# Head sums in one part, the mask on VectorE and an earlier bias transpose in a two-layer transformer kernel

## The chip, the cores and the metric

The kernel runs on one core of a Trainium2 chip. The metric is device time in microseconds (us), the median of several runs. PE is TensorE, DVE is VectorE, ACT is ScalarE, POOL is GpSimd and SP issues most transfers.

## The reference, cut to what matters

Two layers; each is an attention block and a feed-forward block with a residual. 2048 positions, width 1024, 32 heads of 32. The attention is local and dilated: a position looks at 8 keys, 0, 2, ..., 14 positions back.

```python
logits = jnp.einsum("bhsd,bhswd->bhsw", q, kg) * scale      # W = 8 keys per position
logits = jnp.where(mask[None, None, :, :], logits, -1e9)    # keys before the start
attn = _softmax(logits, axis=-1)
o = jnp.einsum("bhsw,bhswd->bhsd", attn, vg)
...
x = x + _A_ref(_layernorm(x), A_wqkv, A_wo)                 # attention
x = x + _B_ref(_layernorm(x), B_w1, B_b1, B_w2, B_b2)       # feed-forward, F = 3584
```

## The kernel before

Positions are handled in 4 groups of 512 per layer. The kernel keeps PE fed: while PE multiplies one group's projections or feed-forward, VectorE prepares another group's attention. For each of 8 chunks `c` VectorE multiplies q with 8 shifted windows of k (`new_prod`, one 128x4096 instruction) and adds the 8 products pairwise. PE then sums over the 4 partitions of each head by a matmul with a 0/1 matrix `smat` (`head_sum`).

```python
def head_sum(n, last=True):
    ...
    first = n % NG == 0
    prod = st[n]["prods"].pop(0)
    for wh in range(2):
        for tb in range(NTT):                       # 4 column groups of PE
            mm(L[tb*H:(tb+1)*H, wh*4:(wh+1)*4, :], lhsT=smat[:], rhs=prod[...],
               start=start, stop=..., tile_position=(0, tb * H))
    if first and last:                              # the mask, as 7 small matmuls
        for w in range(W - 1):
            mm(L[0:H, w, 0:HALO], lhsT=onesrow[:], rhs=maskrow[0:1, w, 0:HALO], ...)

def new_prod(n, c):
    prod = bigp.tile([P, W, T], BF16, name="big")   # 3 buffers
    vec.tensor_tensor(out=prod[:], in0=q chunk c, in1=window of k chunk c, op=ALU.mult)
    ...                                             # add to the others, pairwise
```

With `parts` = 2 (groups 0 and 1 before the change) the products 0 to 3 and 4 to 7 are summed apart, and PE adds the two parts by a second head sum into the same PSUM tile. The order of work is written as stages: a generator issues PE work in units of 8 matmuls, and `sides` hang other work on units. `at(4, f)` issues `f` after unit 4. PE keeps its order; VectorE's order within a stretch is chosen by a scheduler when the program is built, unless `hold()` sets a floor: what is issued later stays behind the last VectorE instruction issued before it.

```python
stage(gen_wo(0, 2))      # output projection of group 0; layernorm tiles 2, 3 are transposed on PE
stage(q2, sides=each(new_prod, 1, 0, 1, 4, 8) + at(3, head_sum, 1, False) + at(4, transpose_late))
...
stage(gen_ffn1(0), sides=at(2, attend, 1) + at(2, spread, 1) + at(2, hold) + ...)

def ln_stats(t, ...):    # VectorE statistics, then two GpSimd instructions
    ...
    vec.bn_aggr(mv[:], stats[:])
    pool.tensor_tensor(out=rstd[:], in0=mv[:, 1:2], in1=eps_t[:], op=ALU.add)
    pool.tensor_tensor(out=rstd[:], in0=rstd[:], in1=mhalf[:], op=ALU.pow)
```

`transpose_late` runs 16 PE transposes: the normalized tiles 2 and 3 of group 0, which the first feed-forward stage needs.

## Time and profile before

| | before |
|---|---|
| time | 1239.82 us (4 runs, 1239.73 to 1239.93) |
| PE busy | 1230.7 us, 99% of the span |
| VectorE busy | 836.5 us, 68% |

The page of the kernel before: the busy row (us, share, instructions), and the chain that ended last, by engine. (In all excerpts from views, lines that do not matter here are left out, also where no dots stand.)

```profile
PE 1230.7 (99%) x5821; PEld 632.5 (51%) x5871; DVE 836.5 (68%) x864; ACT 305.9 (25%) x477; POOL 95.9 (8%) x215
...
PE 99%; issue 0%; ACT 0%; DVE 0%
```

The view of waits, PE alone: who was waited for, us in total, times, longest.

```profile
PE acc L118 <- DVE big L93: 1.1, 1, 1.1
PE acc L118 <- ACT xnT L93: 0.7, 1, 0.7
```

Both waits are in the first 10 us. After that PE hardly stops: the kernel's time is the length of PE's queue.

What the parts of that queue cost is read from start-to-start steps. The timeline of PE (start, length, instruction, operands, count) around group 0's second head sum and mask, the bias transpose, and the stretch at 140 to 151 us:

```profile
36.61 0.18 PE L185 MATMUL acc<-ident,abc 28*128 28x28 bf16 x1
65.20 0.61 PE L118 MATMUL L<-big,smat 128*32 128x512 bf16 x8
65.75 0.33 PE L118 MATMUL L<-maskrow,onesrow 1*32 1x14 bf16 x7
66.01 1.30 PE L118 MATMUL acc<-xnT,wt 128*128 128x512 bf16 x5
147.51 0.61 PE L118 MATMUL L<-big,smat 128*32 128x512 bf16 x8
148.06 1.95 PE L118 MATMUL acc<-xnT,wt 128*128 128x512 bf16 x8
149.84 1.06 PE L215 MATMUL acc<-ident,xn 128*128 128x128 bf16 x16
```

Ordinary 128x512 matmuls start 0.216 us apart. Where a head-sum part stands among them, the stream comes out 0.70 us later, with the mask 0.96 us, around the bias transpose 0.27 us. (Lengths overlap and their ends are modelled, so lengths are not costs.)

The timeline of VectorE and GpSimd before and at the same place. In brackets: idle time before, and what ended it.

```profile
128.62 0.69 DVE L93 TENSOR_TENSOR x<-acc,x 128x512 bf16<-128x512 f32 x1 [2.44 <-PE acc L118]
129.23 2.28 DVE L93 TENSOR_TENSOR big<-qT,kT 128x4096 bf16<-128x4096 bf16 x1
140.70 2.23 DVE L93 TENSOR_TENSOR big<-big 128x4096 bf16<-128x4096 bf16 x1
143.65 0.55 DVE L93 TENSOR_SCALAR xn<-x,mv,rstd 128x1024 bf16<-128x1024 bf16 x1 [0.71 <-POOL rstd L93]
145.90 2.27 DVE L93 TENSOR_TENSOR big<-qT,kT 128x4096 bf16<-128x4096 bf16 x1
149.23 0.55 DVE L93 TENSOR_SCALAR xn<-x,mv,rstd 128x1024 bf16<-128x1024 bf16 x1 [0.93 <-POOL rstd L93]
```

```profile
140.86 2.12 POOL L93 TENSOR_TENSOR rstd<-mv,eps_t 128x1 f32<-128x1 f32 x1 [2.56 <-DVE mv L93]
143.06 0.55 POOL L93 TENSOR_TENSOR rstd<-rstd,mhalf 128x1 f32<-128x1 f32 x1
148.38 0.19 POOL L93 TENSOR_TENSOR rstd<-mv,eps_t 128x1 f32<-128x1 f32 x1 [4.76 <-DVE mv L93]
```

The last normalization (149.23, done at 149.78 us) is ready just before PE's second eight transposes at 149.84 + 0.45 = 150.29 us: half a microsecond of slack. And the same one-column GpSimd addition lasts 2.12 us beside a VectorE addition, 0.19 us without one.

### The profile page before, as it was taken

The page shows a single profiled execution, that of the slowest core. Times are in us where ns is not written, and L with a number is a line of the kernel's source. Part 1 is how long each engine was busy: PE and PEld are TensorE (multiplying, and loading weights), DVE is VectorE, ACT ScalarE, POOL GpSimd, SP SyncE. Part 2 cuts the span into 40 slices and gives each one's busy share as a digit, 9 for nine tenths or more (in the row PEclk, how much of TensorE's full clock was granted, in tenths as well). Part 3 has the DMA queues.
Part 4 walks back from the last instruction along what each step waited for, and adds up shares of the span by engine and source line. Part 5 has one row for each costly group of instructions (what it writes and reads, how often), then busy time and mean ns, then how long its engine had stood idle before and what let it go on. Part 6 is the DMA issues. An engine that isn't in the chain of part 4 may idle for free.

```text
span 1238.2 us, 14051 instructions
## 1 busy us (share of the span) xinstructions
PE 1230.7 (99%) x5821; PEld 632.5 (51%) x5871; DVE 836.5 (68%) x864; ACT 305.9 (25%) x477; POOL 95.9 (8%) x215
## 2 busy tenths in 40 slices
PE   9999999999999999999999999999999999999998
PEld 6666544456444564445644455444654444444444
DVE  7989889996986799337994379843597788012001
ACT  3333252023420144101341023410235001300310
POOL 4010111002000100001000010000001002000000
PEclk9999999999999999999999999999999999999999
DMA  9954564576646556656566565566654568546441
GB/s 300 287 179 139 165 223 134 169 183 211 197 152 205 153 177 169 195 166 178 167 162 196 174 185 157 164 203 198 173 170 134 184 200 205 157 157 195 149 137 54
DMA packets 215328, 219.83 MB, mean 178 GB/s; under 512 B 66066, under 2 KB 184992, under 8 KB 212192
## 3 DMA queue, kind: packets, MB, share of 16 engines
q1 hardware_dynamic: 212592, 208.16, 56.0%
q0 software_dynamic: 2672, 10.76, 2.7%
q8 instruction: 46, 0.75, 0.3%
q14 instruction: 18, 0.15, 0.0%
HBM read 197.40 MB, written 6.29 MB: 165 GB/s over the span
## 4 chain that ended last, share of the span: by engine, by line
PE 99%; issue 0%; ACT 0%; DVE 0%
PE acc L118 99%; PE L L118 0%; PE acc L215 0%; PE L L215 0%; ACT xnT L93 0%; DVE x L93 0%; DVE big L93 0%; PE acc L185 0%
## 5 line engine op out<-in xcount | busy, mean ns | idle before, releaser
L118 PE MATMUL acc<-xnT,wt 128*128 128x512 bf16 (+1 forms) x3376 | 722.4, 376 | 0.7 <-ACT xnT L93 0.7
L118 PEld LDWEIGHTS <-wt 128*128 128x128 bf16 x3376 | 398.0, 119 | 321.2 <-issue 4.3
L118 PE MATMUL acc<-wt,hT 128*128 128x512 bf16 (+1 forms) x1780 | 386.1, 376 | 2.1
L118 PEld LDWEIGHTS <-hT 128*128 128x128 bf16 x1820 | 177.7, 98 | 209.4
L93 DVE TENSOR_TENSOR big<-big 128x2048 bf16<-128x2048 bf16 (+2 forms) x182 | 239.5, 1348 | 1.7
L93 ACT ACTIVATE hT<-acc,b1T 128x512 bf16<-128x512 f32 x224 | 151.6, 687 | 318.5 <-PE acc L118 318.2
L93 DVE TENSOR_TENSOR big<-abc,vT 128x4096 bf16<-128x4096 bf16 x64 | 143.9, 2282 | 48.6 <-DMA abc<-a_d 48.6
L93 DVE TENSOR_TENSOR big<-qT,kT 128x4096 bf16<-128x4096 bf16 x64 | 143.9, 2285 | 24.0 <-ACT kT L93 23.3
L93 DVE TENSOR_TENSOR tmp<-acc,b2bc 128x512 f32<-128x512 f32 x56 | 38.7, 691 | 178.2 <-PE acc L118 174.4
L93 ACT CAST qT<-acc 128x512 bf16<-128x512 f32 x64 | 37.2, 585 | 328.6 <-PE acc L118 328.6
L118 PE MATMUL acc<-wt,oT 128*128 128x512 bf16 x440 | 97.6, 379 | 0.5
L93 DVE BATCH_NORM_STATS2 stats<-x 128x6 f32<-128x512 bf16 x128 | 83.9, 678 | 4.2 <-DMA x<-in_A_x_dram 3.4
L118 PEld LDWEIGHTS <-oT 128*128 128x128 bf16 x448 | 43.8, 98 | 53.1 <-issue 0.3
L93 DVE TENSOR_TENSOR x<-acc,big 128x512 bf16<-128x512 f32 (+1 forms) x9 | 5.7, 632 | 90.0 <-PE acc L118 90.0
L93 ACT CAST vT<-acc 128x512 bf16<-128x512 f32 x64 | 37.5, 586 | 84.9 <-PE acc L118 84.9
L93 ACT CAST kT<-acc 128x512 bf16<-128x512 f32 x64 | 37.5, 585 | 72.1 <-PE acc L118 72.1
L93 POOL TENSOR_TENSOR rstd<-mv,eps_t 128x1 f32<-128x1 f32 x60 | 16.4, 273 | 499.5 <-DVE mv L93 499.4
L93 POOL DMA_DIRECT2D a_d<-a x32 | 18.9, 619 | 406.9 <-DVE a L93 406.9
L93 DVE TENSOR_SCALAR xn<-x,mv,rstd 128x1024 bf16<-128x1024 bf16 x52 | 28.6, 550 | 30.9 <-POOL rstd L93 29.8
L93 DVE TENSOR_TENSOR x<-acc,x 128x512 bf16<-128x512 f32 x64 | 43.0, 671 | 6.3 <-PE acc L118 6.1
L93 DVE TENSOR_TENSOR x<-tmp,x 128x512 bf16<-128x512 f32 x56 | 38.7, 691 | 1.7
L93 POOL TENSOR_TENSOR rstd<-rstd,mhalf 128x1 f32<-128x1 f32 x60 | 33.6, 560 | 4.7
(56 smaller groups left out, 217.3 us busy)
## 6 DMA issues: line engine op xcount, KB each, us to landing
wt<-in_B_w_dram SPq DMA_DIRECT2D x56, 1024.0 KB, 5.8
wt<-in_B_w_dram SPq DMA_DIRECT2D x64, 896.0 KB, 5.0
wt<-in_A_wqkv_dram SPq DMA_DIRECT2D x46, 1024.0 KB, 5.6
wt<-in_A_wo_dram SPq DMA_DIRECT2D x16, 1024.0 KB, 4.9
abc<-a_d POOLq DMA_DIRECT2D x32, 256.0 KB, 5.1
x<-in_A_x_dram SPq DMA_DIRECT2D x16, 256.0 KB, 6.0
out_dram<-x SPq DMA_DIRECT2D x31, 128.0 KB, 1.8
wt<-in_A_wqkv_dram SPq DMA_DIRECT2D x4, 512.0 KB, 7.4
```

Source lines behind the costliest of these rows:

```text
L93: inst = f(*args, **kwargs)
L118: return pe(nc.tensor.matmul(*args, **kwargs))
```

## The change

The intent: take work off the engine that bounds the kernel. Groups 0 and 1 are summed in one part (one more 128x4096 addition on VectorE each, one head-sum part less on PE). The mask is added by VectorE. The bias transpose moves into the first layernorm, where PE waits anyway. Group 1's softmax moves from unit 2 to unit 4, as its products now end later.

```diff
-    maskrow = const.tile([1, W, 16], BF16, name="maskrow")
-    onesrow = const.tile([1, H], BF16, name="onesrow")
+    mask = const.tile([H, W - 1, HALO], F32, name="mask")
 ...
         norm(1)
+        transpose_bias()
 ... (head_sum)
-        if first and last:
-            for w in range(W - 1):
-                mm(L[0:H, w, 0:HALO], lhsT=onesrow[:], rhs=maskrow[0:1, w, 0:HALO], start=False, stop=True, ...)
 ... (attend)
+        if n % NG == 0:
+            vec.tensor_tensor(out=L[0:H, 0:W - 1, 0:HALO], in0=L[0:H, 0:W - 1, 0:HALO], in1=mask[:], op=ALU.add)
 ...
-        stage(gen_qkv(0, 2, qk_next=early), sides=at(14, transpose_bias) + at(14, load_b2) + at(21, head_sum, 0, False))
-        q1 = gen_qkv(1, 2, defer=True, qk_pool=early)
+        stage(gen_qkv(0, qk_next=early), sides=at(14, load_b2))
+        q1 = gen_qkv(1, defer=True, qk_pool=early)
 ...
-        stage(q2, sides=each(new_prod, 1, 0, 1, 4, 8) + at(3, head_sum, 1, False) + at(4, transpose_late))
+        stage(q2, sides=each(new_prod, 1, 0, 1, 4, 8) + at(4, transpose_late))
 ...
-    stage(gen_ffn1(0), sides=at(2, attend, 1) + at(2, spread, 1) + at(2, hold) + ...)
+    stage(gen_ffn1(0), sides=at(4, attend, 1) + at(4, spread, 1) + at(4, hold) + ...)
```

More of the change, by code (lines that the diff above doesn't have):

```diff
@@ L168, in build_constants @@
         pool.affine_select(out=smat[:], in_=smat[:], pattern=[[HP, H]], compare_op=ALU.is_ge, fill=0.0, base=HP - 1, channel_multiplier=-1)
-        pool.memset(maskrow[:], 0.0)
-        for w in range(W):
-            nmask = HALO - DIL * w
-            if nmask > 0:
-                pool.memset(maskrow[0:1, w, 0:nmask], -1e9)
-        pool.memset(onesrow[:], 1.0)
+        pool.memset(mask[:], 0.0)
+        for w in range(W - 1):
+            pool.memset(mask[:, w, 0:HALO - DIL * w], -1e9)
     b1_rows = attp.tile([KF, P], BF16, name="abc")
@@ L289, in head_sum @@
         L = st[n]["L"]
-        first = n % NG == 0
         prod = st[n]["prods"].pop(0)
@@ L295, in head_sum @@
                    rhs=prod[:, wh * 4:(wh + 1) * 4, tb * P:(tb + 1) * P], start=start,
-                   stop=last and not (first and tb == 0), skip_group_check=True, tile_position=(0, tb * H))
-        if first and last:
-            for w in range(W - 1):
-                mm(L[0:H, w, 0:HALO], lhsT=onesrow[:], rhs=maskrow[0:1, w, 0:HALO], start=False, stop=True,
-                   skip_group_check=True, tile_position=(0, 0))
+                   stop=last, skip_group_check=True, tile_position=(0, tb * H))
     def new_prod(n, c):
@@ L537 @@
         stage(gen_wo(0, 2))
-        stage(q2, sides=each(new_prod, 1, 0, 1, 4, 8) + at(3, head_sum, 1, False) + at(4, transpose_late))
+        stage(q2, sides=each(new_prod, 1, 0, 1, 4, 8) + at(4, transpose_late))
     hpool = ctx.enter_context(tc.tile_pool(name="hpool", bufs=1))
-    stage(gen_ffn1(0), sides=at(2, attend, 1) + at(2, spread, 1) + at(2, hold) + each(new_prod, 2, 2, 1, 0, 4) + each(av, 1, 6, 2))
+    stage(gen_ffn1(0), sides=at(4, attend, 1) + at(4, spread, 1) + at(4, hold) + each(new_prod, 2, 2, 1, 0, 4) + each(av, 1, 6, 2))
     stage(gen_ffn2(0), sides=at(0, ln_stats_ahead, 3) + at(15, hold) + each(new_prod, 2, 15, 1, 4, 8) + at(23, hold) + at(23, ln_a, 3, None, True))
```

## The prediction

> **What bounds the kernel now.** TensorE. The page's busy row gives PE 1230.7 of 1238.2 us (99%) and the chain of work that ended last is 99% matmuls. The view of waits shows two stalls of PE, 1.1 and 0.7 us, both in the first 10 us. So what leaves PE's queue counts, and any new wait of PE.
>
> **What leaves PE** (start-to-start steps in the timeline; ordinary 128x512 matmuls are 0.216 us apart):
> - One head-sum part is 8 matmuls in two passes of four that start 3 to 4 ns apart, as the Trainium skill ("TensorE: Matmul & The Clock Gate", Part 3: Packing small matmuls) says of different column groups. With the gaps at entry and exit it delays the stream by 0.70 us (48.97, 147.51 us). One part each of groups 0 and 1 goes: -1.40.
> - The 7 mask matmuls cost 0.26 us (65.75 us), twice (groups 0 and 4): -0.52.
> - The bias transpose cost 0.27 us at 36.6 us. It moves ahead of the first projection matmul, where PE sits idle 0.67 us waiting for ACT's copy; its rows landed by about 6 us. Hidden: -0.27.
> Sum: -2.19 us.
>
> **What enters VectorE.** Two 128x4096 additions of 2.3 us, and two mask additions on 32x98 elements (estimate: 0.2 us each, as VectorE's smallest instructions). 5 us more on an engine 68% busy; it counts only where PE waits for it.
>
> **Where PE might wait.**
> 1. Group 0's head sum. VectorE finishes the products at 61.9 us now, at 64.1 with the extra addition. PE arrives at 65.20 - 0.97 = 64.23. Stall 0 to 0.15 us.
> 2. The PE transposes of layernorm tiles 2 and 3 (149.84 us). The last tile's normalization now ends at 149.78 us and PE takes it at 150.29: slack 0.5. After the change PE arrives 1.9 us earlier (148.4). In the changed program order both additions stand before this normalization, and GpSimd's rstd operations must finish behind them: at 140.86 one lasted 2.12 instead of 0.19 us, until the VectorE addition beside it ended (the Trainium skill, "SBUF — State Buffer", section "SBUF: two separate sides", has this exclusive lock; the trace agrees). Stepping VectorE's new order through with the old durations, the normalization ends at about 149.6 us. PE then stalls about 1.2 us (estimate, 0.3 to 1.8).
> 3. Group 1's head sum, moved two units (3.45 us) later: VectorE done about 158.6, PE there at 160.5. No stall. Group 1's softmax comes some 7 us later, as two products and an addition of group 2 precede it; its value products start 1 to 2 us later, but end 27 us before PE needs them.
> After 160 us nothing on PE waits for VectorE.
>
> **Prediction.** 1239.8 - 2.2 + 1.2 = 1238.8 us, range 1237.4 to 1240.2. Faster by over 2%: 0.005; within 2%: 0.99; slower by over 2%: 0.005.
>
> **What would show it.** PE's matmuls from smat fall from 80 to 64, those from maskrow from 14 to 0. PE reaches the first output projection at 125.3 instead of 126.5 us. In the view of waits a new wait of PE for VectorE's xn, about 1.2 us, stands near 148.4 us; if it is absent the time is about 1237.6. VectorE's busy time rises by 5 us.
>
> **What would make it wrong.** Another interleaving of GpSimd and VectorE before the transposes; bias rows landing late; a transfer late after reordered issues; group 1's softmax blocking ACT's evictions and so PE's accumulators.

## The result, and the profile after

The changed kernel takes 1238.89 us (4 runs, 1238.86 to 1238.93), 0.93 us less than before. The ratio is 0.9992, interval 0.9975 to 1.001: the same, by the 2% measure. Measured again later (experiment 11), it took 1238.76 against 1239.89 us.

Page of the changed kernel, busy row; then PE's waits:

```profile
PE 1231.2 (100%) x5841; PEld 632.9 (51%) x5841; DVE 840.0 (68%) x868; ACT 306.3 (25%) x477; POOL 94.3 (8%) x214
```

```profile
PE acc L118 <- DVE big L93: 1.1, 1, 1.1
PE acc L211 <- DVE xn L93: 1.0, 1, 1.0
PE acc L118 <- ACT xnT L93: 0.6, 1, 0.6
PE acc L211 <- POOL rstd L93: 0.2, 1, 0.2
```

The second line is the new wait. (The last one, which the list before does not have either, stands at 7 us, in the first layernorm.) PE's busy time did not fall although 30 matmuls are gone: some matmul records are missing from each trace, 50 more from the one of before (the counts behind the x show it, 5821 against 5841 for a program with 30 fewer), and ends are modelled. Busy time is not fit for differences of 1 us; steps between starts are.

The timelines after, at the places shown above: PE, then VectorE, then GpSimd.

```profile
147.87 0.61 PE L211 MATMUL acc<-ident,xn 128*128 128x128 bf16 x8
149.50 0.62 PE L211 MATMUL acc<-ident,xn 128*128 128x128 bf16 x8 [1.02 <-DVE xn L93]
149.96 10.53 PE L118 MATMUL acc<-xnT,wt 128*128 128x512 bf16 x48
```

```profile
129.08 0.69 DVE L93 TENSOR_TENSOR x<-acc,x 128x512 bf16<-128x512 f32 x1 [1.04 <-PE acc L118]
131.59 2.24 DVE L93 TENSOR_TENSOR big<-qT,kT 128x4096 bf16<-128x4096 bf16 x1
134.55 0.55 DVE L93 TENSOR_SCALAR xn<-x,mv,rstd 128x1024 bf16<-128x1024 bf16 x1 [0.72 <-POOL rstd L93]
143.57 2.28 DVE L93 TENSOR_TENSOR big<-big 128x4096 bf16<-128x4096 bf16 x1
145.77 0.21 DVE L93 BATCH_NORM_AGGREGATE mv<-stats 128x2 f32<-128x12 f32 x1
145.89 2.29 DVE L93 TENSOR_TENSOR big<-big 128x4096 bf16<-128x4096 bf16 x1
148.89 0.55 DVE L93 TENSOR_SCALAR xn<-x,mv,rstd 128x1024 bf16<-128x1024 bf16 x1 [0.71 <-POOL rstd L93]
```

```profile
146.05 2.18 POOL L93 TENSOR_TENSOR rstd<-mv,eps_t 128x1 f32<-128x1 f32 x1 [4.17 <-DVE mv L93]
148.31 0.55 POOL L93 TENSOR_TENSOR rstd<-rstd,mhalf 128x1 f32<-128x1 f32 x1
```

PE comes to the transposes at 147.87 instead of 149.84 us, 1.97 us earlier. The last normalization is done at 149.44 instead of 149.78, only 0.34 earlier. So the second eight transposes start 1.63 us after the first eight, not 0.45: PE loses 1.18 us there.

The normalization hangs on PE too, through the output projection and the residual additions, and the first of these additions came 1.27 us earlier (127.35 instead of 128.62 us). Where the lead went is shown by the chain that ended last (start, length), between the residual additions and PE's second eight transposes:

```profile
129.08 0.69 DVE x L93
131.76 2.12 POOL rstd L93
143.66 2.19 DVE big L93
146.05 2.19 POOL rstd L93
```

Three long pieces stand in it: an rstd of GpSimd beside the product at 131.59 us, an addition, and an rstd beside the second addition. In the kernel before, that product stood at 129.23 us, between the first two residual additions. Experiments 5 and 12 come back to it.

**Accounting.** Runs differ by up to 0.6 us in when the first projection gets going (the long stretch of 128x256 matmuls starts at 14.42 us before, 14.50 after, between 14.28 and 14.89 in all traces). Why it does was not settled, and it blurs comparisons of 1 us. I therefore use beside the times the *length from the start of that stretch to the end of the span*, one profiled run per kernel: 1223.80 us before, 1222.65 after. The difference, -1.15, is made up of:

| step | us |
|---|---|
| two head-sum parts gone | -1.40 |
| two masks gone | -0.52 |
| bias transpose hidden | -0.27 |
| new stall at the transposes | +1.18 |
| a weight load of the first output projection, late by 0.20 us before and 0.07 after | -0.13 |
| sum | -1.14 |

The last row was not foreseen: before, the second half of those weights landed at 127.52 us and PE's first matmul with it started at 127.56, 0.20 us behind its step.

### The profile page after: what moved, and what is told of

Read it like the earlier page. It is cut to its first block, busy times and chain, and to the rows that moved or that the text cites. A ratio compares the mean times of both kernels' runs of the same rounds, so it can differ in the third digit from the quotient of the medians. Undisturbed runs are those within 1.5% of the kernel's fastest.

```text
span 1237.2 us, 14039 instructions
## 1 busy us (share of the span) xinstructions
PE 1231.2 (100%) x5841; PEld 632.9 (51%) x5841; DVE 840.0 (68%) x868; ACT 306.3 (25%) x477; POOL 94.3 (8%) x214
## 4 chain that ended last, share of the span: by engine, by line
PE 97%; DVE 1%; POOL 1%; DMA 0%; issue 0%; ACT 0%
PE acc L118 97%; POOL rstd L93 1%; DVE stats L93 1%; PE L L118 0%; DVE x L93 0%; DMA x<-in_A_x_dram 0%; DVE xn L93 0%; DVE big L93 0%; PE acc L211 0%; DVE mv L93 0%; PE L L211 0%; ACT xnT L93 0%
## 5 line engine op out<-in xcount | busy, mean ns | idle before, releaser
L93 DVE TENSOR_TENSOR big<-big 128x1024 bf16<-128x1024 bf16 (+2 forms) x184 | 244.2, 1359 | 1.8
```

Source lines behind the costliest of these rows:

```text
L93: inst = f(*args, **kwargs)
```

## The experiments

Lengths are those defined above. "Before there" is the median of the kernel before in the same rounds on the same chip.

| kernel | time, us | before there | length, us | wait at the transposes |
|---|---|---|---|---|
| before | 1239.82 | | 1223.80 | 0 |
| changed | 1238.89 | 1239.82 | 1222.65 | 1.18 |
| e1_norm_first | 1237.94 | 1239.75 | 1221.63 | 0 |
| e2_group1_two_parts | 1239.31 | 1239.75 | 1222.64 | 0.54 |
| e3_rstd_on_vector | 1238.48 | 1239.75 | 1221.95 | 0.55 |
| e4_sum_at_unit2 | 1240.42 | 1239.75 | 1224.14 | 1.15 |
| e5_mask_only | 1240.05 | 1239.96 | 1223.73 | 0.52 |
| e6_bias_only | 1239.75 | 1239.96 | 1223.39 | 0 |
| e7_transpose_unit5 | 1239.38 | 1239.96 | 1223.29 | 0 |
| e8_dma_transpose | 1237.77 | 1239.96 | 1221.60 | none on PE |
| e9_products_early | 1237.67 | 1239.89 | 1221.10 | none on PE |
| e10_sum_at_unit5 | 1236.67 | 1239.89 | 1220.37 | none on PE |
| e11_after_again | 1238.76 | 1239.89 | 1222.57 | 1.15 |
| e12_mask_order_kept | 1239.31 | 1239.88 | 1223.11 | 0 |

The intervals of the ratios are about 0.15% (1.8 us) to each side, so by times alone only e8, e9 and e10 (0.9982, 0.9981 and 0.9974, upper ends 0.9997, 0.9993 and 0.9986) are clearly off the kernel before.

**1. Normalization first.**

```diff
-        stage(gen_wo(0, 2))
-        stage(q2, sides=each(new_prod, 1, 0, 1, 4, 8) + at(4, transpose_late))
+        stage(gen_wo(0, 2), sides=at(0, new_prod, 1, 4))
+        hold()
+        stage(q2, sides=each(new_prod, 1, 0, 1, 5, 8) + at(4, transpose_late))
```

> The changed kernel, but with VectorE's order altered: the product of chunk 4 of group 1 may run at once, all later products and additions of group 1 are held back until the normalization of layernorm tile 3 of group 0. The work is the same. Theory (order): PE's stall before the transposes exists because VectorE puts about 4.6 us of products and additions, and GpSimd's rstd behind them, ahead of that normalization. Then the stall of 1.02 + 0.17 us goes, the normalization ends near 142.6 us, and the time is 1238.89 - 1.2 = 1237.7 us. Rival (load): VectorE simply has too much to do before 160 us; then the stall moves to group 1's head sum at about 159 us and the time stays near 1238.9.

PE's timeline of this run:

```profile
147.87 1.06 PE L211 MATMUL acc<-ident,xn 128*128 128x128 bf16 x16
```

The normalization ended at 143.50 us, the 16 transposes ran in one go, and the length fell by 1.02 us: the work was all there, its order made the stall. The missing 0.2 us came back later: VectorE ended group 1's sum a little after PE got to it, and PE's step there was 0.52 instead of 0.31 us.

**2. Group 1 again in two parts.**

```diff
-        q1 = gen_qkv(1, defer=True, qk_pool=early)
+        q1 = gen_qkv(1, 2, defer=True, qk_pool=early)
 ...  + at(3, head_sum, 1, False), and the softmax back at unit 2
```

> The changed kernel with group 1's head sum put back to two parts and its place as before; group 0, mask and bias stay changed. PE has 0.70 us more before the transposes, so it comes to the second of them at about 149.05 us. VectorE's order there has a product where the changed kernel has the second addition, of the same length, so the normalization should again end at 149.4 us. If the stall is PE coming early to a normalization that did not move, a stall of about 0.4 us is left and the time is 1238.8 us, about that of the changed kernel: group 1's part of the change is worth nothing. If the moved additions made the stall, none is left and the time is 1238.3 us.

Without the second addition in front of it the normalization ended no earlier (149.60 us in a run that started 0.16 us later), as a product took that place. PE had 0.70 us more to do before the transposes and waited 0.54 us instead of 1.18. The length is that of the changed kernel within 0.01 us. So group 1's part of the change took 0.70 us of work from PE and gave back 0.64 as waiting: worth nothing that these lengths can show. It also shows that the second addition is not what made the normalization late: a product in its place did the same. (The product displaced to 131.69 us, with GpSimd's rstd behind it, is on the chain of this run too.) The time, 1239.31 us, is above the expected 1238.8; the stretch began 0.16 us later than in the changed kernel's trace, and the rest is within what the times scatter here (1239.10 to 1240.02).

**3. rstd without GpSimd (wrong result, relative error 0.047).**

```diff
+        if on_vec:                       # tile 3 of group 0 alone
+            vec.tensor_scalar(out=rstd[:], in0=mv[:, 1:2], scalar1=EPS, scalar2=20.0, op0=ALU.add, op1=ALU.mult)
+            return mv, rstd
```

A second edit, not shown, sets a floor that keeps the later products behind this normalization; the order in front of it is that of the changed kernel.

> The changed kernel, but for layernorm tile 3 of group 0 rstd is computed by one small VectorE instruction instead of two GpSimd ones, and the products behind it are held back. [...]a multiplication stands in and the result is wrong on purpose. If the wait for GpSimd behind the addition is 0.7 us of the lateness, the normalization ends about 0.45 us earlier (the small instruction and its semaphores cost 0.25) and the time falls to about 1238.4 us. If GpSimd is not what the normalization waits for, the time stays at 1238.9 us.

VectorE's timeline of this run:

```profile
146.10 2.29 DVE L93 TENSOR_TENSOR big<-big 128x4096 bf16<-128x4096 bf16 x1
148.31 0.15 DVE L93 TENSOR_SCALAR rstd<-mv 128x1 f32<-128x1 f32 x1
148.49 0.55 DVE L93 TENSOR_SCALAR xn<-x,mv,rstd 128x1024 bf16<-128x1024 bf16 x1
```

The normalization starts 0.10 us after the addition's end instead of 0.71; the stall shrinks by 0.63 us and the length by 0.70. Somewhat more than half of the stall is therefore the wait for GpSimd, which could not run beside the addition. The Trainium skill ("SBUF — State Buffer", section "Who interferes with whom") says that a VectorE instruction with two SBUF inputs contends with a GpSimd instruction that reads SBUF; the 2.18 us beside 0.19 us agree.

**4. Group 1's softmax back at unit 2.** The edit: `at(4, ...)` to `at(2, ...)` in the first feed-forward stage.

> The changed kernel with group 1's softmax and head sum back at unit 2 of the first ffn stage instead of 4. Theory: PE comes to the head sum at about 157.0 us, VectorE ends the sum at 158.5, so PE waits 1.5 us more and the time is about 1240.4 us, slower than before the change. Rival: the slack there is large and the move was not needed; then the time stays at 1238.9 us.

The first line of PE's waits:

```profile
PE L L118 <- DVE big L93: 1.5, 1, 1.5
```

A second wait appeared, as expected: 1.5 us at the head sum, length +1.49. The move of the softmax in the change was needed.

**5. The mask alone.** The kernel before with only the mask's edits.

> The kernel before with the mask alone changed: added to the logits by VectorE. PE loses 7 mask matmuls of 0.26 us in all, twice. Expected 1239.82 - 0.52 = 1239.3 us. The rival that small matmuls cost PE nothing because they overlap gives 1239.8 us.

This expectation failed: the length fell by 0.07 us, not 0.52. PE's timeline shows why:

```profile
149.89 0.61 PE L211 MATMUL acc<-ident,xn 128*128 128x128 bf16 x8
150.85 0.62 PE L211 MATMUL acc<-ident,xn 128*128 128x128 bf16 x8 [0.35 <-DVE xn L93]
```

The mask's matmuls did leave: at the first output projection PE is 0.25 us ahead of the kernel before (counted from the long stretch), and the later mask is worth 0.26 again. But at the transposes PE lost 0.52 us. The instruction order of the built program differs there: with the small mask addition in it, the scheduler no longer puts the product of chunk 5 between the first two residual additions (where the kernel before has it, at 129.23 us) but after the statistics of the first tile. VectorE then idles 1.0 us for PE, and GpSimd's rstd waits behind the product. The changed kernel has the same displaced product: the idle 1.04 us at 129.08 and the product at 131.59 in the lines above.

**6. The bias transpose alone.** The kernel before with only that move.

> The kernel before with the bias transpose alone moved into the first layernorm. Expected 1239.82 - 0.27 = 1239.55 us if it hides in PE's 0.67 us wait for ACT; 1239.8 us if it only moves.

Length -0.41: -0.27 for the transpose, and -0.13 because the late weight load of the first output projection cost 0.07 instead of 0.20 us, as in the changed kernel. PE's idle time before the first projection matmul went from 0.67 to 0.56 us in the changed kernel: the transpose is hidden in it.

**7. The PE transposes one unit later.** The edit: `at(4, transpose_late)` to `at(5, transpose_late)`.

> The changed kernel with the 16 PE transposes one unit (8 matmuls, 1.73 us) later. PE then comes to them after the normalization and does not wait for VectorE, but the first ffn matmul follows at once and needs ACT's copies of 1.0 us each: the wait should turn into one of about 1.5 us for ACT. Expected 1239.2 us (1238.9 to 1239.6). If the copies do not hold PE, 1237.7 us.

```profile
149.71 1.06 PE L211 MATMUL acc<-ident,xn 128*128 128x128 bf16 x16
152.38 1.89 PE L118 MATMUL acc<-xnT,wt 128*128 128x512 bf16 x8 [1.61 <-ACT xnT L93]
```

As expected, the wait for VectorE became one for ACT's copies, 1.61 us. A stall on a chain is not removed by starting its last link later.

**8. Tiles 2 and 3 transposed by DMA.** Experiment 1, with `gen_wo(0)` for `gen_wo(0, 2)`.

> The kernel of the first experiment (normalization first), and tiles 2 and 3 transposed by DMA as tiles 0 and 1 are, not on PE. PE loses 16 transposes, 0.90 us. If the last transfer, issued near 142.7 us, lands before PE's first ffn matmul at about 149.6 us, the time is 1237.7 - 0.9 = 1236.8 us; if it lands later, PE waits for the difference (transposing transfers took 4 to 7 us to land in the kernel before, so up to 0.5 us).

The last transfer landed at 147.37 us, in time, and PE lost its 16 transposes. But the time, 1237.77 us, did not fall to the expected 1236.8. The first line of PE's waits:

```profile
PE L L118 <- DVE big L93: 1.1, 1, 1.1
```

PE now came 0.9 us earlier to group 1's head sum, and VectorE's sum was not done until 159.37 us. Everything gained went into a new wait of 1.07 us. This is the same lesson as the change itself, one chain further on.

**9. Two products early.** Experiment 8, with the products of chunks 4 and 5 issued before the output projection (`new_prod(1, 4)`, `new_prod(1, 5, add=False)`) and only the additions behind the hold.

> The DMA-transpose kernel, with the products of chunks 4 and 5 of group 1 both allowed before the first output projection, where VectorE idles about 2 us, and only the additions held back behind the normalization. VectorE then has six instructions (about 13.8 us) between the normalization (about 143.4 us) and the end of group 1's sum, so it ends near 157.1 us, before PE gets there at 158.4. The 1.07 us stall of PE at the head sum seen in the DMA-transpose kernel should vanish: 1237.77 - 1.07 = 1236.7 us. If the stall was not VectorE's amount of work, it stays and the time is 1237.8 us.

The wait at the head sum went, as expected; but another came, the runs scattered (1236.90 to 1238.16), and the time, 1237.67 us, missed the expected 1236.7. The line of PE's waits that is new:

```profile
PE acc L118 <- DMA xnT<-xn: 0.6, 1, 0.6
```

SP's issues in this run (start, length of the issue):

```profile
140.50 1.24 SPq L93 DMA_TRANSPOSE xnT<-xn  x1
141.86 0.50 SPq L93 DMA_DIRECT2D wt<-in_B_w_dram  x1
143.42 2.85 SPq L93 DMA_TRANSPOSE xnT<-xn  x1
```

A 1 MB weight load stands between the two transposing transfers, which it did not in experiment 8 (there the next load was issued at 145.41 us). It landed at 149.10 us and the last transpose at 150.00, against 147.37 in experiment 8. That the load delayed it is read from the order of the landings; no run took the load away.

**10. Group 1's softmax one unit later.** Experiment 8, with `at(5, ...)` for `at(4, ...)`.

> The DMA-transpose kernel with group 1's head sum and softmax one unit (1.73 us) later, at unit 5 of the first ffn stage. PE gets there at 160.1 us, after VectorE's sum at 159.4: the 1.07 us stall should vanish here too, with VectorE's work before it unchanged, and the time be about 1236.7 us. The later softmax has 20 us of slack; if it does not, PE stalls at the output projection of group 1 near 248 us.

PE's waits, all of them:

```profile
PE acc L118 <- DVE big L93: 1.1, 1, 1.1
PE acc L211 <- POOL rstd L93: 1.0, 1, 1.0
PE acc L118 <- ACT xnT L93: 0.6, 1, 0.6
```

They lie in the first 10 us. At 1236.67 us this is the fastest kernel, 3.2 us under the kernel before in the same rounds and 2.1 us under the changed kernel (1238.76), with a correct result.

**11. The changed kernel again**, on the chip of 9 and 10.

> The changed kernel itself, on the chip of these experiments, to compare with on equal terms: 0.9 us under the kernel before, as when first measured (1238.9 us there).

It came out 1.13 us under the kernel before there, against 0.93 when first measured; the stall at the transposes was 1.15 us.

**12. The mask alone, with the order kept.** Experiment 5, with the product of chunk 5 pinned where the kernel before has it.

```diff
+        new_prod(1, 4)
-        stage(gen_wo(0, 2))
+        stage(gen_wo(0, 2), sides=at(0, new_prod, 1, 5, True, False) + at(0, hold))
```

> The mask-only kernel, with the product of chunk 5 of group 1 pinned on VectorE between the first two residual additions of group 0, where the kernel before has it and where the mask-only program no longer does. In the mask-only run the normalization ended at 150.80 us and PE waited about 0.5 us for it. If the displaced product is the cause (VectorE idles 1.1 us for PE and later waits for GpSimd behind the product), the normalization ends about 1 us earlier, the stall goes and the time is 0.5 us under the mask-only kernel: from the first full-width stretch to the end 1223.3 us instead of 1223.7, against 1223.8 before. If the stall comes from something else the mask does, it stays at 1223.7.

```profile
149.64 1.06 PE L211 MATMUL acc<-ident,xn 128*128 128x128 bf16 x16
```

The normalization ended at 149.11 instead of 150.80 us, the transposes ran in one go, and the length is 1223.11, 0.62 under the mask-only kernel and 0.69 under the kernel before (0.52 for the two masks, 0.20 for the late weight load, which cost nothing here). The stall in experiment 5 was the displaced product. (The order is that of the kernel before only as far as this product goes: the addition behind it stands at 140.70 us in the kernel before, ahead of the third tile's normalization, and at 143.18 us here, behind it.) Why the scheduler displaces the product was not looked into.

Counted from the long stretch, the pinned product let the last normalization end 1.57 us earlier than in experiment 5. So the changed kernel with this product in its old place might not stall at all, or by some 0.25 us (estimate: 0.93 us of the 1.27 us lead of its first residual addition is lost before the normalization ends, and would come off the 1.18). No run pinned it there.

## Why the prediction was right

It forecast 1238.8 us and the measured time was 1238.89. The terms, one by one:

- *What leaves PE, -2.19 us.* The matmuls from `smat` fell from 80 to 64 and those from `maskrow` from 14 to 0. PE reached the first output projection at 125.36 us (forecast 125.3). The parts alone bear this out: bias -0.27 (e6), mask -0.52 once its side effect is taken away (e12, e5).
- *Group 0's head sum, stall 0 to 0.15 us.* None was seen.
- *The transposes, stall about 1.2 us.* Measured 1.18 by start-to-start steps; the normalization ended at 149.44 us (forecast about 149.6). Experiment 1 took the stall away by order alone, so the order of VectorE's work, and not its amount, made the stall. The prediction names the two additions before the normalization and GpSimd's rstd behind them, and they are on the chain; experiment 2 shows that a product in place of the second addition does the same. It does not name the displaced product with the first tile's rstd behind it, which is on that chain too and, by the untested estimate under experiment 12, would make most or all of the stall. It stepped VectorE's new order through, so its 149.6 us may hold this.
- *Group 1's head sum, no stall with the softmax moved.* PE came at 160.42 us (forecast 160.5), VectorE was done at 158.50 (158.6). Experiment 4 shows what the move is worth, 1.5 us.
- *Misses of size.* VectorE's busy time rose by 3.5 us, not 5. The value products of group 1 start at 188.18 us against 188.12 before, not 1 to 2 us later. The weight load (-0.13) was not in the sum. None of them moved the total by more than 0.15 us. That the total fits within 0.1 us is partly luck: the start of the first projection alone scatters by 0.6 us.

The net of 0.9 to 1.2 us from 2.2 us of work removed is thus explained: half the gain was given back as a wait, at a place that had only half a microsecond of slack and where VectorE's order had changed (the mask's edit alone changes it, experiment 5). What stays open is the scheduler's reason for moving the product, how much of the stall would be left without that move, and the scatter of 0.6 us in the start of the first projection.

## What to carry to other kernels

When work leaves a saturated engine, it comes earlier to every meeting point with another engine. A producer that this engine feeds comes earlier too while its own order holds (in experiment 6 the last normalization ended 0.40 us earlier, counted from the long stretch, about as much as the length fell), but not when something else is put in its way. So list the slack at each meeting point, with the producer's new order, before counting the gain: waits that are not there yet show only as the distance between a producer's end and its consumer's start. After each removed wait look for the next one (here transposes, then head sum, then a transfer), and move the consumer later or the producer's other work behind it. A small edit can also change the order that a scheduler gives to unrelated instructions; compare the order of the two programs before crediting or blaming the edit.

## What the Trainium skill lacked or had wrong

- "TensorE: Matmul & The Clock Gate", section "Back-to-back issue gap", gives a sustained stream of weight load and matmul about 131 ns per matmul at N=512 and 81 ns at N=128, and calls 216 and 56 ns the isolated gap. Here, at full clock and with a weight load for each matmul, 4916 of 4970 steps behind 128x512 matmuls after 161 us in the changed kernel's trace are 0.21 to 0.22 us, up to 1300 in a row, and the transposes (N=128, 16 in a row) are 0.056 us apart.
- The same page, Part 3, gives the span of packed matmuls but not the cost of going into and out of them: two passes of four 32-column matmuls delay a 128-column stream by 0.70 us, of which two steps of 0.216 us would be 0.43; the 0.27 us left is paid at entry and exit. ("TensorEngine Tiling (Array Packing)" has no time for a change of tiling mode either.) A lone 28x28 transpose in the stream costs 0.27 us, seven 1x14 matmuls behind a head sum 0.26 us.
- "SBUF — State Buffer" has the contention, timed only for a DMA issued from GpSimd; it does not say that a blocked GpSimd instruction shows it as its own length (2.12 and 2.18 us instead of 0.19), nor what the chain here pays: 0.7 us from the end of the VectorE instruction to the start of the one that needs GpSimd's result, 0.55 of it a second GpSimd instruction.
- "DMA: Bandwidth & Descriptors" gives a bandwidth for DMA transposes but no time to landing beside other traffic: in experiment 8 a 128x1024 tile landed 2.7 us after its issue where the issue came before the next 1 MB weight load, and after 6.7 and 3.9 us for the two tiles issued behind it; in experiment 9 after 6.1 and 6.6 us.
